# A second form of the first expert product for superblocks of at most 128 rows

## The chip, the cores and the metric

The kernel runs on one core of one Trainium2 chip. The metric is the device time of one execution in microseconds, lower is better. It is written in Tile, which places all semaphores; the order of the instructions of the part that matters here is the order of the source (manual_schedule).

## The reference

Pooled attention makes x (4608 rows of 512), a dense layer with softplus follows, and then a mixture of eight experts, which is the part of the change:

```python
do_compute = x @ w_skip > 0
e_idx = argmax(x[do_compute] @ w_gate, axis=1)
for e in range(8):
    h = maximum(xc[mask] @ w1[e], 0.0)
    y[mask] = gate_w[mask, None] * (h @ w2[e])
out[do_compute] = xc + y
```

Here w1[e] is 512 x 1024 and w2[e] 1024 x 512. Rows that are not computed are copied.

## The kernel before, in words

The first stage (attention and the dense layer, lines 93 to 734) ends where the experts' first matmul starts, 976.4 us into the span. The rows of each expert are cut into superblocks of at most 256 rows (SB), and a list of superblocks is made on the device. The first ten (list 1, NS1) are full ones that can start early; list 2 holds the rest, unrolled for up to 17 and left when a count n2 is reached (L836). The same word n2 has a bit for each superblock of list 2 that says whether it has more than 128 rows (L321 to L329). Superblocks are numbered through from 0, so list 2 begins with number 10.

A product of two float32 matrices is made of three matmuls: each operand is split into a part rounded to float32r and the rest (h and l), and hh, hl and lh are added in PSUM.

One superblock i (L748 to L807) does in this order:

- POOL issues the indirect DMAs that prepare what follows: w1 of superblock i+1 into raw1 (L759), the rows of i+2 into xg (L763), row numbers of i+3 (L765), and behind split2 w2 of i+1 into raw2 (L770). Where the expert doesn't change, the weights' indices lie out of bounds and nothing is moved.
- If superblock i has another expert than the one before, split2 (L388 to L394) makes w2h (ACT) and w2l (DVE) from raw2 in four pieces, inside a conditional (L767).
- The hidden product: 4 pairs of 128 features, each with 2 x 12 matmuls of 128x128 weights (w1h or w1l stationary) against 256 columns of x (L780). A pair ends in one PSUM tile h of the pool ps_f, which has four buffers; ACT makes hh with Relu (L784) and DVE hl (L785).
- turn(i+1) (L360 to L371): eight transposes of the next superblock's rows on PE, two copies to xth on ACT (L369), two subtractions to xtl on DVE (L370).
- If superblock i+1 has another expert, split1 (L380 to L386) makes w1h and w1l in four pieces, inside a conditional (L790).
- For each half j of 128 rows, the second product: 24 matmuls with 128 columns of hh or hl stationary and 512 columns of w2h or w2l moving (L799 to L801), a last sum on DVE (L803), and the indirect DMA of 128 rows to out on POOL (L805). In list 2 the second half stands inside a conditional on the bit (L795).

The program stands once for every superblock. Every engine with work in a conditional tests it itself; the page and the views put such instructions at lines like L767, L790, L793, L795 and L836, as COMPARE_BRANCH, ALU_OP and EVENT_SEMAPHORE on an engine's queue (PEldq, ACTq, DVEq, POOLq).

Of the kernel before, what the change touches and what calls it, by code (L numbers as in the profile page):

```python
# [9 lines left out]
F32 = mybir.dt.float32  # L10
# [4 lines left out]
AF = mybir.ActivationFunctionType  # L15
ALU = mybir.AluOpType
# [4 lines left out]
P = 128  # L21
# [7 lines left out]
SB = 256  # L29
# [5 lines left out]
def tile_kernel(ctx, tc, qT, kT, vT, wbits, w9, w1, w2, out):  # L35
    nc = tc.nc
# [23 lines left out]
    ident = const.tile([P, P], F32, name="ident")  # L60
# [37 lines left out]
    ws = {}  # L98
# [106 lines left out]
    misc = [None, 0]  # L205
# [134 lines left out]
    xg, xth, xtl = [None] * 3, [None] * 2, [None] * 2  # L340

    def at(i):
        return (lists[1], i) if i < NS1 else (lists[2], i - NS1)
# [8 lines left out]
    def gather(i):  # L352
        rows = NTOK - G if i < NS1 else NTOK
        for j in range(2):
            nc.gpsimd.indirect_dma_start(  # L355
                out=xg[i % 3][j], out_offset=None, in_=x2d[:rows, :],
                in_offset=bass.IndirectOffsetOnAxis(ap=ids[i % 4][:, j:j + 1], axis=0),
                bounds_check=rows - 1, oob_is_err=False)

    def turn(i, ps, tag):  # L360
        for half in range(2):
            tr = ps.tile([P, 512], F32, tag=tag, name="tr").rearrange("p (a b) -> p a b", a=2)
            for k2 in range(2):
                kk = half * 2 + k2
                for j in range(2):
                    nc.tensor.transpose(tr[:, k2, j * P:(j + 1) * P],  # L366
                                        xg[i % 3][j][:, kk * P:(kk + 1) * P], ident)
            h = xth[i % 2][:, half * 2:half * 2 + 2, :]
            nc.scalar.activation(out=h, in_=tr, func=AF.Copy)  # L369
            nc.vector.tensor_tensor(out=xtl[i % 2][:, half * 2:half * 2 + 2, :], in0=tr,  # L370
                                    in1=h.bitcast(F32), op=ALU.subtract)  # L371

    def fetch(name, src, i):
        li, s = at(i)
        nc.gpsimd.indirect_dma_start(  # L375
            out=ws[name], out_offset=None, in_=src,
            in_offset=bass.IndirectOffsetOnAxis(ap=li["widx"][:, s:s + 1], axis=0),
            bounds_check=NE * P - 1, oob_is_err=False)
# [18 lines left out]
    def wtile(name, *shape, dtype=F32):  # L397
        return wpool.tile([P, *shape], dtype, tag="w", name=name)

    with ExitStack() as ph:  # L400
# [10 lines left out]
        for i in range(2):  # L411
            t = ep.tile([P, 2 * SP], F32, name=f"kbd{i}")
# [229 lines left out]
        wl = load_weights()  # L642
# [72 lines left out]
        for i in range(2):  # L715
            t = xp.tile([P, 4 * G], F32R, tag="xl" if i == 0 else "xh", name=f"xt{i}")
            t = t[:, :4 * SB].rearrange("p (a b) -> p a b", a=4)
# [4 lines left out]
        hs = wtile("hs", 2, 8, SB, dtype=F32R)  # L722
        hh, hl = hs[:, 0], hs[:, 1]
# [3 lines left out]
        t = xp.tile([P, 4 * G], F32, tag="xl", name="xg1")  # L727
# [9 lines left out]
    ps_t = ctx.enter_context(tc.tile_pool(name="ps_t", bufs=2, space=PSUM))  # L737
    ps_f = ctx.enter_context(tc.tile_pool(name="ps_f", bufs=4, space=PSUM))
# [4 lines left out]
    t = ex.tile([P, 2 * XW], F32, name="xg2")  # L743
    xg[2] = [t[:, j * XW:(j + 1) * XW] for j in range(2)]
    nc.gpsimd.memset(t, 0.0)
    ys = [ex.tile([P, D], F32, name=f"ys{j}") for j in range(2)]

    def superblock(i, cond, mask, more, big=None):  # L748

        _, s = at(i)  # L750

        def changes(s_):
            return (mask & (1 << s_)) > 0

        with ExitStack() as st:
            if cond is not None:
                st.enter_context(tc.If(cond))
            if more > 0:
                fetch("raw1", w1, i + 1)  # L759
            if i == 0 and more > 0:  # L760
                gather(1)
            if more > 1:
                gather(i + 2)  # L763
            if more > 2:
                load_ids(i + 3)  # L765
            if i > 0 and i != NS1 - 1:
                with tc.If(changes(s)):  # L767
                    split2()
            if more > 0:
                fetch("raw2", w2, i + 1)  # L770
            xh, xl = xth[i % 2], xtl[i % 2]
            for fp in range(4):
                h = ps_f.tile([P, 2, SB], F32, tag="h", name="h")
                for f2 in range(2):
                    f0 = (fp * 2 + f2) * P
                    n = 0
                    for kk in range(4):
                        wh, wl = ws["w1h"][:, kk, f0:f0 + P], ws["w1l"][:, kk, f0:f0 + P]
                        for l, r in ((wh, xh), (wh, xl), (wl, xh)):
                            nc.tensor.matmul(h[:, f2, :], lhsT=l, rhs=r[:, kk, :],  # L780
                                             start=n == 0, stop=n == 11)
                            n += 1
                fs = slice(fp * 2, fp * 2 + 2)
                nc.scalar.activation(out=hh[:, fs, :], in_=h, func=AF.Relu)  # L784
                nc.vector.scalar_tensor_tensor(out=hl[:, fs, :], in0=h, scalar=0.0,  # L785
                                               in1=hh[:, fs, :].bitcast(F32),
                                               op0=ALU.max, op1=ALU.subtract)
            if more > 0:
                turn(i + 1, ps_t, "t")
                with tc.If(changes(s + 1)):  # L790
                    split1()
            for j in range(2):
                with ExitStack() as half:  # L793
                    if j and big is not None:
                        half.enter_context(tc.If((big & (32 << s)) > 0))  # L795
                    y = ps_o.tile([P, D], F32, tag=f"y{j}", name=f"y{j}")
                    js = slice(j * P, (j + 1) * P)
                    for f in range(8):
                        nc.tensor.matmul(y, lhsT=hh[:, f, js], rhs=ws["w2h"][:, f, :], start=f == 0, stop=False)  # L799
                        nc.tensor.matmul(y, lhsT=hh[:, f, js], rhs=ws["w2l"][:, f, :], start=False, stop=False)  # L800
                        nc.tensor.matmul(y, lhsT=hl[:, f, js], rhs=ws["w2h"][:, f, :], start=False, stop=f == 7)  # L801
                    r = xg[i % 3][j]
                    nc.vector.scalar_tensor_tensor(out=ys[j], in0=y, scalar=r[:, D:D + 1],  # L803
                                                   in1=r[:, :D], op0=ALU.mult, op1=ALU.add)
                nc.gpsimd.indirect_dma_start(  # L805
                    out=out, out_offset=bass.IndirectOffsetOnAxis(ap=ids[i % 4][:, j:j + 1], axis=0),
                    in_=ys[j], in_offset=None, bounds_check=NTOK - 1, oob_is_err=False)  # L807
# [77 lines left out]
```

## Time and profile before

| | us |
|---|---|
| median of 3 runs | 1439.58 |
| lowest and highest | 1439.39 to 1444.45 |
| profiled execution | 1446.33 |
| its span | 1444.6 |

The profile is of one execution. Start times count from the start of its span; 1.7 us of the profiled execution lie around the span. A matmul's duration is its latency: back-to-back matmuls overlap, so their cost is read from start to start. The granted clock of TensorE over the span is 0.998 of the full one.

### The profile page before, as it was taken

Reading aid. Unit: us, or ns where it says so; the run is one execution under the profiler, and the core shown is the slowest. Engines: PE = TensorE matmul, PEld = TensorE weight load, DVE = VectorE, ACT = ScalarE, POOL = GpSimd, SP = SyncE. Lnnn points to the kernel's source line nnn. Section 1 sums busy time; section 2 is a strip of 40 time slices with the busy share of each in tenths; the row PEclk is TensorE's granted clock in tenths of the full one; section 3 lists DMA queues with packets and bytes.
Section 4 is the critical chain, followed back from the end, with each engine's and each line's share of the span. In section 5 each row is a group of like instructions: output and inputs, shape, how many; then the busy total and the mean of one; then the engine's idle time right before and its main releaser. Section 6 shows DMA issues by size and latency. Waiting matters only on the chain. (4 is left out here: it accounts for less than half of the span.)

```text
span 1444.6 us, 21443 instructions
## 1 busy us (share of the span) xinstructions
PE 1402.9 (97%) x7434; PEld 1156.7 (80%) x7434; DVE 843.1 (58%) x2053; ACT 647.8 (45%) x1204; POOL 309.0 (21%) x365
## 2 busy tenths in 40 slices
PE   5999999999999999999999999999999999999996
PEld 3666877777877777777777777889898989999896
DVE  7898784784783883963963945753453422224254
ACT  5888654555554554555555444551111111113142
POOL 2010021021011121121120020134242433323232
PEclk9999999999999999999999999999999999999999
DMA  5445231231140130230310200502122111114051
GB/s 204 155 153 175 87 106 48 54 105 34 46 122 24 60 108 25 71 96 25 90 61 8 81 31 18 186 25 75 52 60 74 46 46 45 52 36 163 25 225 67
DMA packets 57691, 114.19 MB, mean 79 GB/s; under 512 B 17205, under 2 KB 23477, under 8 KB 56544
## 3 DMA queue, kind: packets, MB, share of 16 engines
q1 hardware_dynamic: 40032, 76.07, 17.0%
q0 software_dynamic: 17536, 36.60, 7.6%
q8 instruction: 62, 1.02, 0.3%
q14 instruction: 61, 0.50, 0.1%
HBM read 166.14 MB, written 29.67 MB: 136 GB/s over the span
## 5 line engine op out<-in xcount | busy, mean ns | idle before, releaser
L617 PE MATMUL h<-xh,wt 128*128 128x512 f32 x1152 | 390.4, 399 | 1.5 <-ACT wt L462 0.6
L617 PEld LDWEIGHTS h<-xh,wt 128*128 128x128 f32 x1152 | 216.6, 189 | 61.1 <-issue 11.5
L118 DVE CUSTOM_DVE_ANT_0 junk<-rows,w9b 128x512 bf16<-128x512 f32 x324 | 230.8, 712 | 10.2 <-ACT rows L112 3.8
L638 PE MATMUL y<-wt,gh 128*128 128x512 f32 x576 | 231.4, 402 | 2.4 <-ACT gh L625 2.2
L780 PE MATMUL h<-xt,w1h 128*128 128x256 f32 x1280 | 229.1, 281 | 2.7 <-PEq L793 1.0
L617 PE MATMUL h<-xl,wt 128*128 128x512 f32 x576 | 228.1, 396 | 0.0
L640 PE MATMUL y<-wt,gl 128*128 128x512 f32 x576 | 227.9, 396 | 0.0
L639 PE MATMUL y<-wt,gh 128*128 128x512 f32 x576 | 227.8, 396 | 0.0
L780 PEld LDWEIGHTS h<-xt,w1h 128*128 128x128 f32 x1280 | 198.3, 190 | 5.1 <-issue 1.4
L623 DVE SCALAR_TENSOR_TENSOR a<-h,a 128x512 f32<-128x512 f32 x144 | 99.0, 688 | 175.3 <-ACT a L622 169.5
L784 ACT ACTIVATE hs<-h 128x512 fp32r<-128x512 f32 x80 | 47.8, 598 | 330.8 <-PE h L780 268.8
L620 ACT ACTIVATE a<-h 128x512 f32<-128x512 f32 x144 | 86.2, 599 | 236.0 <-PE h L617 219.7
L780 PE MATMUL h<-xt,w1l 128*128 128x256 f32 x640 | 179.9, 281 | 0.7 <-DVEq L830 0.7
L531 POOL TENSOR_TENSOR q<-q,st 64x144 f32<-64x144 f32 (+7 forms) x60 | 60.7, 1019 | 533.4 <-DVE st L530 172.0
L625 ACT ACTIVATE gh<-a 128x512 fp32r<-128x512 f32 x144 | 90.8, 630 | 105.7 <-DVE a L623 103.9
L785 DVE SCALAR_TENSOR_TENSOR hs<-h,hs 128x512 fp32r<-128x512 f32 x80 | 54.6, 691 | 141.6 <-ACT hs L784 129.5
L638 PEld LDWEIGHTS y<-wt,gh 128*128 128x128 f32 x576 | 108.3, 188 | 29.0 <-ACT gh L625 3.3
L640 PEld LDWEIGHTS y<-wt,gl 128*128 128x128 f32 x576 | 108.3, 188 | 26.6 <-DVE gl L627 0.6
L617 PEld LDWEIGHTS h<-xl,wt 128*128 128x128 f32 x576 | 108.6, 189 | 23.5 <-issue 1.9
L639 PEld LDWEIGHTS y<-wt,gh 128*128 128x128 f32 x576 | 108.4, 188 | 23.6
L780 PEld LDWEIGHTS h<-xt,w1l 128*128 128x128 f32 x640 | 121.5, 190 | 0.9 <-DVEq L830 0.9
L799 PE MATMUL y<-w2h,hs 128*128 128x512 f32 x304 | 120.3, 396 | 0.4 <-ACT hs L784 0.4
(181 smaller groups left out, 1973.8 us busy)
## 6 DMA issues: line engine op xcount, KB each, us to landing
w9b<-w SPq DMA_DIRECT2D x81, 256.0 KB
raw<-wbits SPq DMA_DIRECT2D x32, 512.0 KB
x2d<-rows SPq DMA_DIRECT2D x36, 260.0 KB
kv<-kT SPq DMA_DIRECT2D x28, 288.0 KB
kv<-vT SPq DMA_DIRECT2D x28, 288.0 KB
q<-qT SPq DMA_DIRECT2D x8, 224.0 KB
q<-qT SPq DMA_DIRECT2D x8, 192.0 KB
q<-qT SPq DMA_DIRECT2D x8, 160.0 KB
```

Source lines behind the costliest of these rows:

```text
L118: nc.vector.tensor_tensor_reduce(out=ws["junk"], in0=rows[t][:, :D], in1=w9b[e], scale=1.0, scalar=0.0, op0=ALU.mult, op1=ALU.add, accum_o ...
L531: nc.gpsimd.tensor_tensor(out=ep_, in0=ep_, op=ALU.mult, in1=rc[:tp, h].unsqueeze(2).to_broadcast([tp, 2 * nt, SP]))
L617: nc.tensor.matmul(h, lhsT=l, rhs=r[:, kk, :], start=n == 0, stop=n == 11)
L620: nc.scalar.activation(out=a, in_=h, func=AF.Abs)
L623: nc.vector.scalar_tensor_tensor(out=a, in0=h, scalar=0.0, in1=a, op0=ALU.max, op1=ALU.add)
L625: nc.scalar.activation(out=gh, in_=a, func=AF.Copy)
L638: nc.tensor.matmul(y, lhsT=th, rhs=wh, start=c == 0, stop=False)
L639: nc.tensor.matmul(y, lhsT=th, rhs=wl, start=False, stop=False)
L640: nc.tensor.matmul(y, lhsT=tl, rhs=wh, start=False, stop=c == 15)
L780: nc.tensor.matmul(h[:, f2, :], lhsT=l, rhs=r[:, kk, :], start=n == 0, stop=n == 11)
L785: nc.vector.scalar_tensor_tensor(out=hl[:, fs, :], in0=h, scalar=0.0, in1=hh[:, fs, :].bitcast(F32), op0=ALU.max, op1=ALU.subtract)
L799: nc.tensor.matmul(y, lhsT=hh[:, f, js], rhs=ws["w2h"][:, f, :], start=f == 0, stop=False)
```

## The change

The hidden product moves into a function hidden, as it was. A second function, hidden_small, takes the 128 rows of x as the stationary operand and 512 features of w1 as the moving one, 24 matmuls in all, and leaves the Relu of the result, rows on partitions, in hr, a free part of the tile misc. hidden_turn then transposes hr in eight pieces of 128x128 and makes hh and hl from the PSUM tiles. List 1 calls hidden, as before. In list 2 each superblock has two conditionals on the bit: one with hidden and turn, one with hidden_small, turn and hidden_turn.

```diff
--- before.py
+++ after.py
@@ -745,6 +745,53 @@
     nc.gpsimd.memset(t, 0.0)
     ys = [ex.tile([P, D], F32, name=f"ys{j}") for j in range(2)]
 
+    hr = misc[0][:, 3072:4096].rearrange("p (a b) -> p a b", b=P)
+    assert misc[1] <= 1024
+
+    def hidden(i):
...
+    def hidden_small(i):
+
+        xh, xl = xth[i % 2], xtl[i % 2]
+        for half in range(2):
+            h = ps_f.tile([P, 4, P], F32, tag="h", name="hs")
+            fs = slice(half * 512, half * 512 + 512)
+            n = 0
+            for kk in range(4):
+                wh, wl = ws["w1h"][:, kk, fs], ws["w1l"][:, kk, fs]
+                for l, r in ((xh, wh), (xl, wh), (xh, wl)):
+                    nc.tensor.matmul(h.rearrange("p a b -> p (a b)"), lhsT=l[:, kk, :P], rhs=r,
+                                     start=n == 0, stop=n == 11)
+                    n += 1
+            nc.scalar.activation(out=hr[:, half * 4:half * 4 + 4, :], in_=h, func=AF.Relu)
+
+    def hidden_turn():
+        for half in range(2):
+            fs = slice(half * 4, half * 4 + 4)
+            tr = ps_f.tile([P, 4, P], F32, tag="h", name="ht")
+            for f in range(4):
+                nc.tensor.transpose(tr[:, f, :], hr[:, half * 4 + f, :], ident)
+            nc.scalar.activation(out=hh[:, fs, :P], in_=tr, func=AF.Copy)
+            nc.vector.tensor_tensor(out=hl[:, fs, :P], in0=tr, in1=hh[:, fs, :P].bitcast(F32),
+                                    op=ALU.subtract)
+
     def superblock(i, cond, mask, more, big=None):
 
         _, s = at(i)
@@ -768,25 +815,22 @@
                     split2()
             if more > 0:
                 fetch("raw2", w2, i + 1)
...
+            if big is None:
+                hidden(i)
+                if more > 0:
+                    turn(i + 1, ps_t, "t")
+            else:
+
+                with tc.If((big & (32 << s)) > 0):
+                    hidden(i)
+                    if more > 0:
+                        turn(i + 1, ps_t, "t")
+                with tc.If((big & (32 << s)) < 1):
+                    hidden_small(i)
+                    if more > 0:
+                        turn(i + 1, ps_t, "t")
+                    hidden_turn()
             if more > 0:
-                turn(i + 1, ps_t, "t")
                 with tc.If(changes(s + 1)):
                     split1()
             for j in range(2):
```

## Rows read from the trace of the kernel before

**Rows 1.** The page, busy time, share of the span and instructions.

```profile
PE 1402.9 (97%) x7434; PEld 1156.7 (80%) x7434; DVE 843.1 (58%) x2053; ACT 647.8 (45%) x1204; POOL 309.0 (21%) x365
```

**Rows 2.** The page, costliest groups: line, operation, shapes, count | busy us, mean ns | idle before.

```profile
L780 PE MATMUL h<-xt,w1h 128*128 128x256 f32 x1280 | 229.1, 281 | 2.7 <-PEq L793 1.0
...
L784 ACT ACTIVATE hs<-h 128x512 fp32r<-128x512 f32 x80 | 47.8, 598 | 330.8 <-PE h L780 268.8
...
L799 PE MATMUL y<-w2h,hs 128*128 128x512 f32 x304 | 120.3, 396 | 0.4 <-ACT hs L784 0.4
```

**Rows 3.** Timeline of PE, superblocks 17, 18, start of 19: start us, us, instruction [idle, releaser].

```profile
1373.12 0.40 PE L780 MATMUL h<-xt,w1h 128*128 128x256 f32 x2
...
1384.44 1.03 PE L366 MATMUL tr<-ident,xg 128*128 128x128 f32 x8
...
1385.23 0.48 PE L799 MATMUL y<-w2h,hs 128*128 128x512 f32 x1
...
1390.57 0.39 PE L801 MATMUL y<-w2h,hs 128*128 128x512 f32 x1
...
1391.98 0.48 PE L780 MATMUL h<-xt,w1h 128*128 128x256 f32 x2 [1.02 <-PEq L793]
...
1409.69 0.39 PE L801 MATMUL y<-w2h,hs 128*128 128x512 f32 x1
...
1411.06 0.47 PE L780 MATMUL h<-xt,w1h 128*128 128x256 f32 x2 [0.98 <-ACT w1h L384]
```

**Rows 4.** Timeline, PE and DVE, superblock 19.

```profile
1423.36 0.40 PE L801 MATMUL y<-w2h,hs 128*128 128x512 f32 x1
...
1423.51 1.28 DVE L370 TENSOR_TENSOR xt<-tr,xt 128x512 fp32r<-128x512 f32 x2
```

**Rows 5.** Line 790 in superblock 19: duration ns min/median/max, first and last start.

```profile
L790 DVEq EVENT_SEMAPHORE  x1: 21/21/21, 1424.8 to 1424.8; - x1
```

**Rows 6.** Line 793 at the end of superblock 17, PE's queue.

```profile
L793 PEldq COMPARE_BRANCH  x1: 210/210/210, 1386.8 to 1386.8; - x1
...
L793 PEldq EVENT_SEMAPHORE  x1: 51/51/51, 1391.0 to 1391.0; - x1
```

**Rows 7.** Timeline, waits released by another engine's conditional, superblocks 10 and 18.

```profile
1210.78 0.39 PE L780 MATMUL h<-xt,w1l 128*128 128x256 f32 x1 [0.67 <-DVEq L830]
...
1391.14 3.90 ACT L392 ACTIVATE w2h<-raw 128x1024 fp32r<-128x1024 f32 x4 [1.09 <-PEq L793]
```

**Rows 8.** Line 767 at the head of superblock 17, DVE's queue.

```profile
L767 DVEq EVENT_SEMAPHORE  x1: 21/21/21, 1374.1 to 1374.1; - x1
```

**Rows 9.** Timeline, ACT, DVE and POOL, superblocks 17 to 19.

```profile
1385.18 1.08 ACT L369 ACTIVATE xt<-tr 128x512 fp32r<-128x512 f32 x2
...
1393.07 4.63 DVE L393 TENSOR_TENSOR w2l<-raw,w2h 128x1024 fp32r<-128x1024 f32 x4 [0.53 <-DVEq L793]
...
1398.89 1.05 POOL L375 DMA_INDIRECT raw<-w,misc  x1 [0.30 <-ACT hs L784]
...
1407.57 3.91 ACT L384 ACTIVATE w1h<-raw 128x1024 fp32r<-128x1024 f32 x4
...
1414.58 2.01 ACT L392 ACTIVATE w2h<-raw 128x1024 fp32r<-128x1024 f32 x2 [3.10 <-DMA raw<-w,misc]
```

**Rows 10.** Stretches: length, busy us (count) by engine, granted clock, DMA share, GB/s.

```profile
1388.00:1390.00 2.00, 2.00 (x11) 1.65 (x10) 2.00 (x3) 2.00 (x3) 0.00 (x0) 1.00 0.52 221
...
1412.00:1414.00 2.00, 2.00 (x20) 2.00 (x20) 1.97 (x3) 0.00 (x0) 0.00 (x0) 1.00 0.23 90
...
1438.00:1440.00 2.00, 0.00 (x0) 0.00 (x0) 0.00 (x0) 0.00 (x0) 0.00 (x0) 0.53 0.02 4
```

**Rows 11.** Groups by shape, line 507 (scores; boot is the start of the kernel).

```profile
L507 PE MATMUL s<-kbd,q 128*128 128x144 f32 x128 | 18.4, 286 | 0.0
...
L507 PE MATMUL s<-kbd,boot 128*128 128x144 f32 x32 | 9.1, 466 | 14.0 <-ACT raw L456 6.9 <-ACT kbd L504 5.1 <-DVE boot L520 2.0
```

**Rows 12.** Chain of waits, list 2: an output of 128 rows.

```profile
1414.25 2.34 DMA out<-ys,ids
```

More of the change, by code (lines that the diff above doesn't have):

```diff
@@ L746, in tile_kernel @@
     ys = [ex.tile([P, D], F32, name=f"ys{j}") for j in range(2)]
+    hr = misc[0][:, 3072:4096].rearrange("p (a b) -> p a b", b=P)
+    assert misc[1] <= 1024
+    def hidden(i):
+        xh, xl = xth[i % 2], xtl[i % 2]
+        for fp in range(4):
+            h = ps_f.tile([P, 2, SB], F32, tag="h", name="h")
+            for f2 in range(2):
+                f0 = (fp * 2 + f2) * P
+                n = 0
+                for kk in range(4):
+                    wh, wl = ws["w1h"][:, kk, f0:f0 + P], ws["w1l"][:, kk, f0:f0 + P]
+                    for l, r in ((wh, xh), (wh, xl), (wl, xh)):
+                        nc.tensor.matmul(h[:, f2, :], lhsT=l, rhs=r[:, kk, :],
+                                         start=n == 0, stop=n == 11)
+                        n += 1
+            fs = slice(fp * 2, fp * 2 + 2)
+            nc.scalar.activation(out=hh[:, fs, :], in_=h, func=AF.Relu)
+            nc.vector.scalar_tensor_tensor(out=hl[:, fs, :], in0=h, scalar=0.0,
+                                           in1=hh[:, fs, :].bitcast(F32),
+                                           op0=ALU.max, op1=ALU.subtract)
+    def hidden_small(i):
+        xh, xl = xth[i % 2], xtl[i % 2]
+        for half in range(2):
+            h = ps_f.tile([P, 4, P], F32, tag="h", name="hs")
+            fs = slice(half * 512, half * 512 + 512)
+            n = 0
+            for kk in range(4):
+                wh, wl = ws["w1h"][:, kk, fs], ws["w1l"][:, kk, fs]
+                for l, r in ((xh, wh), (xl, wh), (xh, wl)):
+                    nc.tensor.matmul(h.rearrange("p a b -> p (a b)"), lhsT=l[:, kk, :P], rhs=r,
+                                     start=n == 0, stop=n == 11)
+                    n += 1
+            nc.scalar.activation(out=hr[:, half * 4:half * 4 + 4, :], in_=h, func=AF.Relu)
[8 more added lines that the diff above has]
+                                    op=ALU.subtract)
     def superblock(i, cond, mask, more, big=None):
@@ L770, in superblock @@
                 fetch("raw2", w2, i + 1)
[L771 to L787, printed above, removed]
+            if big is None:
[12 more added lines that the diff above has]
+                    hidden_turn()
             if more > 0:
-                turn(i + 1, ps_t, "t")
                 with tc.If(changes(s + 1)):
```

## The prediction

> **What bounds the kernel now.** I read the page's busy table first: PE is busy 97% of the span [rows 1], so a gain must shorten PE's own row of work, and a loss comes from anything that opens a gap in it. The table of costliest groups then counts what the changed part runs: 1280 first-product matmuls are 64 to a superblock (w1h against two halves of x), so 20 superblocks, and 304 matmuls at L799 are 8 to a half, so 38 halves: two superblocks run one half [rows 2]. The timeline shows which: 17 and 18 have one y half between their hidden products [rows 3]. Only they can take the new short form. Superblocks 10 to 16 and 19, eight of them, are in the second list too: they get both new tests and keep the old work. Superblocks 0 to 9 are untouched.
>
> **The short form, PE alone.** Superblock 17's hidden product takes 1373.12 to 1384.44, 11.3 us, the eight transposes of turn 0.79, the 24 y matmuls of 512 columns 5.34 from first to last start, 0.23 each [rows 3]. The new product is 24 matmuls of that width, 24 x 0.23 = 5.5, and eight more 128x128 transposes, 0.8. Saved on PE alone: 11.3 - 6.3 = 5.0 a superblock, 10 us in all. That is the ceiling.
>
> **The eight big superblocks.** This is where I think the change loses. A conditional body that is skipped still has to raise the semaphores that its work would have raised. The trace shows it as an EVENT_SEMAPHORE on each engine that has work in the body, and it fires in order, when that engine has finished what came before. At the end of superblock 17 PE tested L795's condition at 1386.8, four microseconds early, but its event waited until 1391.0, when the last y matmul was through [rows 6], and the next matmul began 1.02 us after the drain [rows 3]. Others wait for such events: split2's first copy on ACT was released by PE's event of L793, and PE at superblock 10 by DVE's event of L830 [rows 7]. After the change hh and hl are written last, in program order, by hidden_turn inside the second conditional. In a big superblock that body is skipped, so y's first matmuls must wait for ACT's and DVE's events there, and those come only when ACT and DVE are through with everything in the first body, turn's copies included. Today's L790 events are the same point: in superblock 19 DVE's is at 1424.8 [rows 5], right behind the turn subtraction that ends at 1424.79 [rows 4]. The first y matmul that reads hl started at 1423.36 [rows 4]; it would start just after 1424.8, 1.45 us later, plus 0.1 to 0.2 for the weight load that can no longer be pulled ahead (at L830 PE started 0.06 us after the event). I take 1.6. The bounds are 0.8 (PE's own drain alone: the 1.02 seen, less the further tests that follow it there) and 1.75. Nothing hides it, since PE has no other gap in these superblocks for it to replace. 8 x 1.6 = 12.8 us. Behind the waiting weight load queue the rest of y and the next product on PE, and behind them DVE's last sum, the output's DMA and the next fetches on POOL: all of it moves later together. In a big superblock the first body ends in a jump, as L793's body does wherever it is taken, and that shows no gap; it costs nothing while PE's sequencer runs ahead.
>
> **Superblock 17.** The first body is skipped. The PSUM tiles of the short form take the places of the skipped h tiles, so PE waits for ACT's and DVE's events. DVE has just finished y's last sum of superblock 16; its event at L767 is at 1374.1 [rows 8], the new one some 0.3 later: PE starts at 1374.5 instead of 1373.12. Product to 1380.0, turn to 1380.8, new transposes to 1381.6. ACT does the second Relu (0.6 [rows 2]), two turn copies, then the first new copy (0.54 each, half of the 1.08 for two [rows 9]), until 1382.4; DVE the two turn subtractions (1.28 for two [rows 4]) and the first new one, until 1383.5. y's third matmul starts at 1383.6, the last 21 x 0.23 later at 1388.4, against 1390.57 [rows 3]. Gain 2.2, of 5.0.
>
> **Superblock 18.** It changes expert, so ACT and DVE do split2 at its head, ahead of the new test in their program. PE waits for their events behind that. raw2's traffic stops at 1389.0 (52% of the stretch from 1388 [rows 10]); for superblock 19 ACT, which waited for the data, started 2.1 us after the traffic ended (1414.58 against 23% of the stretch from 1412 [rows 9, 10]), so I take 1391.1 as the landing, just where ACT starts today [rows 7]. The shorter 17 does not bring it forward, since its fetch was issued at 17's head. DVE follows the first copy by some 1.1 and needs 4.63 for its four pieces [rows 9]: done at 1396.9. PE then starts at 1397.1 instead of 1391.98. By 17's pattern (13.9 us from first to last matmul) the last y matmul starts at 1411.0, against 1409.69 [rows 3]: 1.3 later, all that 17 won and more. Superblock 19 starts that much later; its weights come earlier than now, as POOL's queue follows 17's output.
>
> PE would stand idle for 8 us in front of superblock 18. The granted clock shows the price: when PE has no work left the clock is 0.53 from 1438 on, down at the lower of its levels (1.2 against 2.4 GHz) [rows 10]. At the start of the kernel the score matmuls after such pauses take 466 ns, the same form later 286 [rows 11], though the clock column has 1.00 there. Bounds: nothing, or all 24 matmuls at half speed, 5.5; I take 2.0, a little over a third of them. By the clock column at the start nothing would be lost, and the sum below would be 14.1. The Trainium skill ("TensorE: Matmul & The Clock Gate", Part 1) says that the throttled state is the default and that activity releases it; by that rule the matmuls at the start, and the first ones behind this wait, run slow whatever the column says. The 466 against 286 ns agree with the rule, the column does not.
>
> **Sum.** 12.8 - 2.2 + 3.5 + 2.0 = 16.1 us later. The profiled execution took 1446.33 (span 1444.6), the median of the runs is 1439.58, so the profiled one is 6.7 above; I put the difference on the median: 1455.6. About 0.5% (7.2 us) is what a measurement of this kernel can tell from no change.
>
> **Rivals.**
> *The skipped bodies cost only their tests (chance 0.10).* No event is waited for, by PE or from it. Then 17 and 18 win 5.0 each, less 1.5 each because y waits for the last copies, and 19 waits for its weights: their fetch, behind 17's output on POOL, is issued at 1398.89 today [rows 9], 3.5 earlier then; it lands within 8.7 (split1 begins at 1407.57 [rows 9]), and 2.3 for the first piece on ACT and DVE make 1406.4, where PE would be ready at 1411.06 - 7.0 = 1404.1. Net -7.0 + 2.3 = -4.7: 1434.9, not slower; at best, with the weights in time and the copies hidden, -10, and half of this chance I put beyond the bound of 0.5%. The tests are free while PE's sequencer is ahead (4 us at L793). Against: rows 6 and 7. It decides if y's first matmul in a big superblock follows turn's transposes without a gap. The Trainium skill ("Advanced Engine Details and Errata", Control Flow Timing) gives about 108 ns for a compare-and-branch; by it alone 20 tests would be an estimated 2.2 us, and the change would come out 2.5 us ahead. The rows say otherwise, as the gap is made by the event and not by the test.
>
> *PE drains, but nobody else is waited for (0.13).* 8 x 0.8 = 6.4, less the 4.7: +1.7, 1441.3. For it: the 1.0 gap of PE behind L793 is sure [rows 3, 6]. Against: PE's wait for DVE at L830 [rows 7].
>
> *Each skip leaves the fetched code (0.11).* The skipped bodies are 80 and 208 PE instructions long; L793's is 48 and shows no more than the drain. If PE must fetch code after each skip, at the 2.3 us of a small transfer in the chain [rows 12], some 1.5 us of it beyond the wait eight times and 2.3 twice, this adds 16.6: 1472.
>
> *The change does not do what it says:* excluded, since the two one-half superblocks are there, and the bit that skips their second half is the one the new tests read.
>
> **Numbers.** The forecast has 0.66 and its own range is 1451 (1.45 a superblock, no clock loss, raw2 1.6 earlier: 11.6 - 2.2 + 1.9) to 1460 (1.75, and the clock for all 24: 14.0 - 2.2 + 9.0). The range 1441 to 1470 also takes in the drain case and the lower part of the fetch case. Slower by over 0.5%: 0.65 of the forecast and 0.11, 0.76. Within: 0.13, half of the first rival and the forecast's edge, 0.19. Faster: 0.05.
>
> **What would show it.** In the timeline of superblocks 10 to 16, a gap of some 1.6 us on PE between turn's transposes and y's third matmul, released by DVE's event of the second new test; in 17 a late start of 1.4 and last y start near 1388 plus the 11.2 of the seven before; in 18 a PE gap of about 8 us that ends with split2's last subtraction, with a granted clock below 1.00. The prediction is wrong if the big superblocks keep their length, or if 18's product starts before split2 is over. If the gaps are longer than 3 us and no engine's event ends them, it is the fetch.

## The result, and the profile after

The kernel after takes 1461.53 us (median of 4 runs, 1460.85 to 1462.35) against 1441.75 before (4 runs, 1439.39 to 1444.45): a ratio of 1.014, with the interval from 1.012 to 1.016, so slower by 17 to 23 us. The profiled execution took 1460.85, its span is 1458.9.

The place is the second list. I measure it from the last y start of superblock 9 to that of superblock 19, in the timeline of PE: 241.5 us against 224.1, 17.4 more. The rest of the two spans differs by 3 us the other way, in work that the change doesn't touch. The table gives the lengths of the list and of four superblocks for every kernel of this study, in its profiled execution, each from one last y start to the next; the ratio is that to the kernel before on the same chip.

| kernel | 11 (big) | 17 (short) | 18 (short) | 19 (big) | list 2 | ratio, 95% interval |
|---|---|---|---|---|---|---|
| before | 23.12 | 17.68 | 19.12 | 23.90 | 224.1 | |
| after | 24.72 | 15.65 | 25.01 | 26.14 | 241.5 | 1.014 (1.012 to 1.016) |
| first_only | 23.12 | 17.68 | 19.23 | 24.44 | 224.9 | 0.999 (0.998 to 1.001) |
| second_full | 24.70 | 19.27 | 21.37 | 28.27 | 243.7 | 1.012 (1.008 to 1.016) |
| second_short | 24.70 | 19.26 | 21.36 | 29.86 | 245.3 | 1.012 (1.009 to 1.015) |
| second_no_hh | 24.21 | 18.68 | 20.34 | 26.84 | 236.0 | 1.009 (1.006 to 1.012) |
| turn_behind | 23.58 | 14.98 | 24.86 | 24.62 | 231.6 | 1.005 (1.003 to 1.007) |
| split2_inside | 24.93 | 16.16 | 22.16 | 28.93 | 243.6 | 1.014 (1.011 to 1.017) |
| both | 23.72 | 15.26 | 20.35 | 26.67 | 230.1 | 1.005 (1.003 to 1.007) |
| else_form | 24.05 | 14.12 | 17.02 | 29.92 | 231.2 | 1.005 (1.003 to 1.006) |
| else_turn | 23.14 | 13.36 | 16.66 | 29.83 | 223.5 | 0.9995 (0.998 to 1.001) |
| else_turn_out | 23.12 | 13.36 | 18.18 | 24.64 | 219.7 | 0.995 (0.994 to 0.997) |
| warm | 24.84 | 16.39 | 22.92 | 28.33 | 242.7 | one run |
| before_out | 23.12 | 17.68 | 19.06 | 24.30 | 224.5 | 1.000 (0.999 to 1.001) |

The page of the kernel after, busy times:

```profile
PE 1399.9 (96%) x7306; PEld 1146.2 (79%) x7306; DVE 840.7 (58%) x2049; ACT 647.5 (44%) x1204; POOL 309.5 (21%) x365
```

Against [rows 1] PE has 128 matmuls fewer, two times 96 - 24 - 8, and 3 us less to do, and the span is 14.3 longer. The time lies in gaps. The waits of PE in the second list name them (total us, times, longest):

```profile
PE hs L780 <- DVEq L824: 9.9, 2, 8.5
PE y L843 <- ACTq L828: 6.8, 8, 0.9
PE y L845 <- DVEq L828: 1.8, 8, 0.2
```

Lines 824 and 828 are the two new conditionals. Eight times, once in each big superblock, y's first and third matmul wait for events of the second one; twice the short product waits for an event of the first one. Superblock 12 in the timeline of PE and DVE, and the rows of line 828 there (duration in ns, first and last start):

```profile
1268.85 1.03 PE L366 MATMUL tr<-ident,xg 128*128 128x128 f32 x8
1270.28 1.28 DVE L370 TENSOR_TENSOR xt<-tr,xt 128x512 fp32r<-128x512 f32 x2
1270.72 0.50 PE L843 MATMUL y<-w2h,hs 128*128 128x512 f32 x1 [0.84 <-ACTq L828]
...
1271.67 0.50 PE L845 MATMUL y<-w2h,hs 128*128 128x512 f32 x1 [0.23 <-DVEq L828]
```

```profile
L828 ACTq EVENT_SEMAPHORE  x1: 17/17/17, 1270.7 to 1270.7; - x1
...
L828 DVEq EVENT_SEMAPHORE  x1: 21/21/21, 1271.6 to 1271.6; - x1
```

In [rows 3] y starts 0.79 behind the transposes; here it is 1.87, when ACT's event has come, and the third matmul starts at 1271.67, when DVE's has. DVE's event stands right behind the turn subtraction, which ends at 1271.56. The body of line 828 is skipped here. Nobody works in it, and still everyone who reads hh or hl waits until ACT and DVE have finished what is in front of it.

The timeline of PE, superblocks 17, 18 and the start of 19:

```profile
1381.25 0.39 PE L845 MATMUL y<-w2h,hs 128*128 128x512 f32 x1
1383.02 0.71 PE L780 MATMUL hs<-w1h,xt 128*128 128x512 f32 x2 [1.39 <-DVEq L824]
...
1388.70 1.03 PE L366 MATMUL tr<-ident,xg 128*128 128x128 f32 x8
...
1396.90 0.39 PE L845 MATMUL y<-w2h,hs 128*128 128x512 f32 x1
1405.77 1.19 PE L780 MATMUL hs<-w1h,xt 128*128 128x512 f32 x2 [8.48 <-DVEq L824]
...
1421.91 0.39 PE L845 MATMUL y<-w2h,hs 128*128 128x512 f32 x1
1423.51 0.47 PE L761 MATMUL h<-xt,w1h 128*128 128x256 f32 x2 [1.20 <-issue]
```

The gap of 8.48 us in front of 18 is the largest of the kernel's second list. DVE's row for split2, and the events of the first conditional's line, say what ends it:

```profile
1400.94 4.63 DVE L393 TENSOR_TENSOR w2l<-raw,w2h 128x1024 fp32r<-128x1024 f32 x4 [0.93 <-ACT w2h L392]
```

```profile
L824 DVEq EVENT_SEMAPHORE  x2: 21/21/21, 1382.9 to 1405.6; - x2
```

split2's last subtraction ends at 1405.57, the event comes at 1405.6, PE starts at 1405.77. And stretches there, with the granted clock as the third number from the end:

```profile
1400.00:1402.00 2.00, 0.00 (x0) 0.00 (x0) 1.07 (x2) 2.00 (x3) 1.04 (x1) 0.65 0.07 25
1402.00:1404.00 2.00, 0.00 (x0) 0.00 (x0) 2.00 (x3) 1.75 (x2) 0.21 (x1) 0.50 0.16 60
1408.00:1410.00 2.00, 2.00 (x6) 1.57 (x5) 0.00 (x0) 0.00 (x0) 1.41 (x2) 0.50 0.88 336
1412.00:1414.00 2.00, 2.00 (x12) 1.64 (x11) 0.00 (x0) 0.05 (x1) 0.00 (x0) 1.00 0.92 384
```

The clock falls to the lower level (1.2 against 2.4 GHz) while PE stands, and is still there from 1408 to 1410: there the matmuls follow each other at 0.43 us, and from 1411 on at 0.23. (The twelve of the last row include the first short transposes.)

### The profile page after: what moved, and what is told of

It reads as the page before. It is cut to its first block, busy times and chain, and to the rows that moved or that the text cites. A ratio compares the mean times of both kernels' runs of the same rounds, so it can differ in the third digit from the quotient of the medians.

```text
span 1458.9 us, 21336 instructions
## 1 busy us (share of the span) xinstructions
PE 1399.9 (96%) x7306; PEld 1146.2 (79%) x7306; DVE 840.7 (58%) x2049; ACT 647.5 (44%) x1204; POOL 309.5 (21%) x365
## 5 line engine op out<-in xcount | busy, mean ns | idle before, releaser
L617 PEld LDWEIGHTS h<-xh,wt 128*128 128x128 f32 x1152 | 216.6, 189 | 60.9 <-issue 11.3
L761 PE MATMUL h<-xt,w1h 128*128 128x256 f32 x1152 | 206.5, 281 | 1.9 <-issue 1.2
L620 ACT ACTIVATE a<-h 128x512 f32<-128x512 f32 x144 | 86.2, 599 | 235.9 <-PE h L617 219.7
L761 PEld LDWEIGHTS h<-xt,w1h 128*128 128x128 f32 x1152 | 178.7, 190 | 3.9 <-issue 1.6
L765 ACT ACTIVATE hs<-h 128x512 fp32r<-128x512 f32 x72 | 43.1, 599 | 309.8 <-PE h L761 269.6
L761 PE MATMUL h<-xt,w1l 128*128 128x256 f32 x576 | 162.0, 281 | 0.7 <-DVEq L874 0.7
L843 PE MATMUL y<-w2h,hs 128*128 128x512 f32 x304 | 120.3, 396 | 7.7 <-ACTq L828 6.8
L845 PE MATMUL y<-w2h,hs 128*128 128x512 f32 x304 | 119.6, 393 | 2.2 <-DVEq L828 1.8
L847 DVE SCALAR_TENSOR_TENSOR ys<-y,xg 128x512 f32<-128x512 f32 x38 | 28.5, 751 | 161.1 <-PE y L845 161.1
```

Source lines behind the costliest of these rows:

```text
L617: nc.tensor.matmul(h, lhsT=l, rhs=r[:, kk, :], start=n == 0, stop=n == 11)
L620: nc.scalar.activation(out=a, in_=h, func=AF.Abs)
L761: nc.tensor.matmul(h[:, f2, :], lhsT=l, rhs=r[:, kk, :], start=n == 0, stop=n == 11)
```

## The experiments

The theory: a conditional body that is skipped costs its in-order events, 1.6 us in each big superblock through the second new conditional, and the wait for split2 in 18 through the first. The rivals: each engine pays for fetching code behind a skip, by the length of the body; only PE's drain costs; the tests cost; or the short form itself is slow. The edits below are against the kernel after, unless another is named.

**first_only: one conditional, always entered.** The second one and its body are left out, so the short superblocks do the long form's work.

```diff
-                with tc.If((big & (32 << s)) > 0):
+                with tc.If((big & 31) > 0):
                     hidden(i)
...
-                with tc.If((big & (32 << s)) < 1):
-                    hidden_small(i)
...
-                    hidden_turn()
```

> In list 2 one conditional that is always entered stands around the hidden product and turn, and there is no second one; every superblock takes the old 256-column form. Theory (only a skipped body costs, because its events come late): the ten entered conditionals cost nothing, and the time is that of the kernel before within 2 us, near 1442, with no gap between turn's transposes and y. Rival (the tests and the jump out of a body cost, or the loss of the finer waits at the end of any conditional): 0.8 to 1.6 us a superblock on ten superblocks, 8 to 16 us more, 1450 to 1458.

Superblock 11 takes 23.12 us, to the hundredth that of before, and the ratio is 0.999. The timeline of PE there:

```profile
1245.25 1.04 PE L366 MATMUL tr<-ident,xg 128*128 128x128 f32 x8
1246.04 0.48 PE L838 MATMUL y<-w2h,hs 128*128 128x512 f32 x1
```

0.79 between the two, as in [rows 3]. Here a test and a body that is entered cost nothing that can be measured.

**second_full, second_short, second_no_hh: a second conditional that is never entered.** In all three hidden and turn run unconditionally in every superblock; the skipped body is the whole short form, or hidden_turn alone, or hidden_small alone, which writes neither hh nor hl.

```diff
-                with tc.If((big & (32 << s)) > 0):
-                    hidden(i)
...
+                hidden(i)
+                if more > 0:
+                    turn(i + 1, ps_t, "t")
-                with tc.If((big & (32 << s)) < 1):
+                with tc.If((big & 31) > 30):
                     hidden_small(i)
                     if more > 0:
                         turn(i + 1, ps_t, "t")
                     hidden_turn()
```

> In list 2 the old hidden product and turn stand unconditionally; behind them stands one conditional that is never entered, with the whole new body (short product, turn, transposes and copies to hh and hl). No superblock uses the short form. Theory: y's first matmuls wait in all ten superblocks for ACT's and DVE's events of the skipped body, 1.6 us each, 16 us more than before: about 1458. Rival drain (only PE's own event): 0.8 each, 1450. Rival fetch (code behind a long skip): 16 us too, but then the next kernel, with a short body, falls to 1450.

> As the kernel with the never entered second conditional, but its body is only the eight new transposes with their copies to hh and hl, 16 PE instructions instead of some 80. No superblock uses the short form. Theory (events of ACT and DVE, which come when turn's copies are through, however long the body): unchanged, 1.6 us in each of ten superblocks, about 1458, the gap before y's third matmul released by DVE's event. Rival fetch: the skip is short, so the gap falls to PE's drain, 0.8 each, about 1450.

> As the kernel with the never entered second conditional, but its body is only the short product with its Relu into hr: nothing in it writes hh or hl, which y reads. 48 PE instructions are skipped. No superblock uses the short form. Theory: y no longer waits for ACT's or DVE's events, only PE's own event is left, which comes when turn's last transpose is through: some 0.8 us in each of ten superblocks, 8 us more than before, about 1450. Rival (the waits of y are not what costs, any skip costs the same): 16 us, 1458. Rival (PE's event costs nothing): 1442.

The full body and the short one both give 24.70 in superblock 11. So the length of the skipped body doesn't matter there, and code fetching is out. Their timelines of PE there show the two waits of the kernel after; second_short first, then second_full:

```profile
1246.24 0.50 PE L839 MATMUL y<-w2h,hs 128*128 128x512 f32 x1 [0.84 <-ACTq L827]
...
1247.19 0.50 PE L841 MATMUL y<-w2h,hs 128*128 128x512 f32 x1 [0.22 <-DVEq L827]
```

```profile
1247.81 0.50 PE L842 MATMUL y<-w2h,hs 128*128 128x512 f32 x1 [0.84 <-ACTq L827]
...
1248.77 0.50 PE L844 MATMUL y<-w2h,hs 128*128 128x512 f32 x1 [0.22 <-DVEq L827]
```

Without a write of hh and hl in the body 24.21 are left: the wait for ACT and DVE is gone, and PE's own drain remains. It is 1.09 us, not 0.8, and the list is 11.9 longer than before where I expected 8. The timeline of PE, and PE's rows of line 827 (the skipped conditional) and line 830 (split1's, which comes next):

```profile
1247.98 1.03 PE L366 MATMUL tr<-ident,xg 128*128 128x128 f32 x8
1249.68 0.47 PE L839 MATMUL y<-w2h,hs 128*128 128x512 f32 x1 [0.67 <-DVE hs L766]
```

```profile
L827 PEldq EVENT_SEMAPHORE  x1: 51/51/51, 1249.1 to 1249.1; - x1
```

```profile
L830 PEldq COMPARE_BRANCH  x1: 215/215/215, 1249.3 to 1249.3; - x1
```

The releaser that the timeline names is not the one: that subtraction ended at 1249.55 and writes hl, which y's first matmul doesn't read, and in superblocks 11 to 18 y starts 0.17 us behind the end of line 830's test, however far from the subtraction. PE tested line 827 at 1246.9, ahead of its work, but its event came when the transposes were through, 1249.1, and only then could it test line 830, 1249.3, with 0.2 us for the test. So a test is free as long as PE's sequencer is ahead, and not free behind an event.

Superblock 19 stands apart in all three: 28.27, 29.86 and 26.84 against 23.90. ACT's last Relu comes late there, and with it y. In second_short it starts 3.1 us behind the first transpose (0.3 in the kernel before), and y waits longest:

```profile
1439.38 0.50 PE L839 MATMUL y<-w2h,hs 128*128 128x512 f32 x1 [3.71 <-ACTq L827]
```

In second_full and second_short the clock also falls behind this wait (0.50 from 1442 to 1444 in second_full). Why the Relu is late is not shown, and for 19 no rival is excluded.

**turn_behind: the turn behind both conditionals.**

```diff
                     hidden(i)
-                    if more > 0:
-                        turn(i + 1, ps_t, "t")
                 with tc.If((big & (32 << s)) < 1):
                     hidden_small(i)
-                    if more > 0:
-                        turn(i + 1, ps_t, "t")
                     hidden_turn()
+                if more > 0:
+                    turn(i + 1, ps_t, "t")
```

> The changed kernel with turn(i+1) taken out of both conditionals of list 2 and put behind them. In a big superblock the events of ACT and DVE in the skipped second body then come when the last Relu and its remainder are through, some 1.7 us after the last product matmul, while PE drains and does turn's transposes (0.8). Theory: y no longer waits for them, PE's own drain of 1.1 us (the body that writes no hh: 24.20 against 23.12 us a superblock) is what stays, so eight big superblocks lose 1.1 instead of 1.6, 4 us less than the changed kernel, and the two short ones gain some 0.8 each, since ACT makes hh before turn's copies: near 5 to 6 us less than the changed kernel, 1.0% above the kernel before instead of 1.4%. Rival (the waits do not hang on turn's copies): the same as the changed kernel.

Superblock 11 takes 23.58, the whole ratio is 1.005: half of what I expected to be left. The timeline of PE in superblock 12:

```profile
1268.45 1.06 PE L366 MATMUL tr<-ident,xg 128*128 128x128 f32 x8 [0.30 <-PEq L826]
1269.27 0.48 PE L841 MATMUL y<-w2h,hs 128*128 128x512 f32 x1
```

ACT's and DVE's events now come before the turn copies and are covered by the eight transposes, as no wait for them is left in front of y. PE's drain is still there, but costs 0.46 and not 1.1, since the transposes stand directly behind the event with no test between, and the next test runs under them. Superblock 18 keeps its gap (8.94 us, by DVE's event of line 824).

**split2_inside: split2 in the first body, and behind the short form in the second.** raw2's fetch, which may overwrite what split2 reads, goes behind both.

```diff
-            if i > 0 and i != NS1 - 1:
-                with tc.If(changes(s)):
-                    split2()
-            if more > 0:
-                fetch("raw2", w2, i + 1)
...
                 with tc.If((big & (32 << s)) > 0):
+                    with tc.If(changes(s)):
+                        split2()
                     hidden(i)
...
                     hidden_turn()
+                    with tc.If(changes(s)):
+                        split2()
+                if more > 0:
+                    fetch("raw2", w2, i + 1)
```

> The changed kernel with split2 of list 2 moved into the two bodies: ahead of the old product in the first, behind hidden_turn in the second, and the fetch of raw2 behind both. Theory: in superblock 18 DVE's event of the skipped first body no longer stands behind split2, so PE's gap there falls from 8.5 to some 1.4 us, as in superblock 17, the clock is not lost (24 matmuls in 5.7 instead of 7.9 us), and y of 18 is paced by split2 instead; 18 gets 6 to 8 us shorter, the big superblocks keep their 1.6. The fetch for superblock 19 is issued later, which may give back 1 to 3. Sum: 4 to 8 us less than the changed kernel, 0.9 to 1.1% above the kernel before. Rival (the gap in 18 is the wait for the weights themselves, wherever the split stands): PE idle moves in front of y and the time stays within 2 us of the changed kernel.

I expected 4 to 8 us less than the kernel after, and there are none: 1.014 again. PE in front of 18, then at 18's y, then POOL's fetch of raw2 for 19:

```profile
1404.20 0.70 PE L780 MATMUL hs<-w1h,xt 128*128 128x512 f32 x2 [3.07 <-DVEq L824]
```

```profile
1415.17 0.50 PE L849 MATMUL y<-w2h,hs 128*128 128x512 f32 x1 [1.89 <-ACT w2h L392]
```

```profile
1420.56 1.23 POOL L375 DMA_INDIRECT raw<-w,misc  x1 [7.05 <-ACT w1h L384]
```

The gap of 8.48 is 3.07 (DVE's event now stands behind split1's last piece and 17's last sum), and the clock fell all the same: 0.50 from 1406 to 1408, and the 24 matmuls took 7.17 us. split2 then stands in front of y instead, which waits 1.89 for it. 18 wins 2.85. But 17 loses 0.5 and each big superblock 0.2, because w2l has a conditional writer behind the second test too, and 19 loses 2.8, because raw2's fetch for it goes out only at 1420.56, 2.4 us ahead of 18's last y start (11.0 ahead in the kernel after, at 1410.89): y's second matmul waits 1.30 for DVE's event behind that late split2, and the clock is 0.50 once more from 1440 to 1442. The work was moved from one wait into four others. The rival had this time, within 2 us of the kernel after, and PE's idle in front of y; but the gap in front of 18 did shrink.

**both: the two edits together.**

> The two moves together: split2 inside the bodies, turn and the fetch of raw2 behind both conditionals. Theory: the two gains add, 10 to 13 us less than the changed kernel, 0.3 to 0.6% above the kernel before; the eight drains of PE (1.1 each, 9 us) are left and are more than the two short superblocks win. Rival (drains are free once nothing else waits): below the kernel before by up to 5 us.

1.005, as turn_behind alone. Of the 4.5 us that 18 wins over turn_behind, 2.05 are lost in 19, 0.3 in 17 and 0.1 in each of the seven big ones ahead of it; the list is 1.5 shorter, which the ratio can't show. With two plain conditionals the change stays slower than before.

**else_form: the second conditional as the first one's Else.**

```diff
-                with tc.If((big & (32 << s)) > 0):
+                with tc.If((big & (32 << s)) > 0) as cmp:
...
-                with tc.If((big & (32 << s)) < 1):
+                with cmp.Else():
```

> The changed kernel with the second conditional written as the Else of the first, nothing else. One engine then runs either body and is brought to a common count at the end. Theory: events are still needed where the bodies differ in their counts, PE at least has to make up the difference, and y has to wait for a count that holds for both bodies; between the kernel before plus 9 us (drain alone) and the changed kernel. If the events come only on the path with the smaller count (the short one), the big superblocks lose nothing and the time is at or below the kernel before. The timeline of superblocks 10 to 16 decides: 24.7, 24.2 or 23.1 us each.

This separates the events from the rest. The trace has no EVENT_SEMAPHORE on either line, and the short product of 17 starts with no gap. The timeline of PE in 11, and at the head of 17, 18 and 19:

```profile
1240.94 0.50 PE L843 MATMUL y<-w2h,hs 128*128 128x512 f32 x1 [0.30 <-ACT xt L369]
```

```profile
1373.23 0.63 PE L780 MATMUL hs<-w1h,xt 128*128 128x512 f32 x2
...
1389.10 0.70 PE L780 MATMUL hs<-w1h,xt 128*128 128x512 f32 x2 [1.59 <-ACT w1h L384]
...
1407.58 0.51 PE L761 MATMUL h<-xt,w1h 128*128 128x256 f32 x2 [3.05 <-ACT w1h L384]
```

17 and 18 are now 3.6 and 2.1 below before. But big superblocks keep 0.9, since y's first matmul waits for turn's first copy on ACT (0.30 of idle) and its third, 0.84 behind it, for turn's first subtraction on DVE. And 19 loses 6: its weights aren't there when the shorter 18 ends, and then the clock falls:

```profile
1410.00:1412.00 2.00, 2.00 (x11) 2.00 (x11) 2.00 (x2) 0.37 (x1) 0.00 (x0) 0.50 0.56 229
```

**else_turn: the Else form, and the turn behind both bodies.** This is else_form with the diff of turn_behind.

> The Else form with turn(i+1) behind it. In the Else form a big superblock took 24.05 us (23.13 before) and y waited for turn's copies on ACT, with no event and no drain of PE; the short superblocks started without waiting for events, and 18 kept its clock (24 matmuls in 5.6 us). Theory: with turn behind, y and turn wait for the last Relu and its remainder at most, which come while turn's transposes run: 0 to 0.5 us a big superblock instead of 0.9, so 0 to 4 us, against 3 to 5 us won by the two short ones: between 0.3% below and 0.1% above the kernel before. Rival (a wait at the end of the Else costs PE a drain wherever it stands): 0.5 and more a superblock, 0.2 to 0.4% above the kernel before, as with two conditionals and turn behind.

Now a big superblock takes 23.14 and costs nothing, 17 wins 4.3 and 18 wins 2.5. The ratio is still 0.9995: 19 takes 29.83, 5.9 more than before. Its wait in the timeline of PE, the stretch behind it, and POOL's issues of 17's second output and of the fetch for 19's first weights:

```profile
1401.49 0.51 PE L761 MATMUL h<-xt,w1h 128*128 128x256 f32 x2 [4.01 <-ACT w1h L384]
```

```profile
1403.00:1405.00 2.00, 2.00 (x10) 2.00 (x11) 2.00 (x3) 1.28 (x2) 0.00 (x0) 0.50 0.95 401
```

```profile
1389.22 1.82 POOL L847 DMA_INDIRECT out<-ys,ids  x1 [2.54 <-DVE w2l L393]
1391.34 1.04 POOL L375 DMA_INDIRECT raw<-w,misc  x1 [0.30 <-ACT hs L791]
```

The fetch stands on POOL behind the output of 17's empty second half, and that issue waited 2.54 us. (The row names split2 on DVE; in second_full and split2_inside the same issue waits 2.46, and the row names the landing of the first output.)

**else_turn_out: the output's DMA inside the half's own conditional.** The empty half then issues none.

```diff
-                nc.gpsimd.indirect_dma_start(
-                    out=out, out_offset=bass.IndirectOffsetOnAxis(ap=ids[i % 4][:, j:j + 1], axis=0),
-                    in_=ys[j], in_offset=None, bounds_check=NTOK - 1, oob_is_err=False)
+                    nc.gpsimd.indirect_dma_start(
+                        out=out, out_offset=bass.IndirectOffsetOnAxis(ap=ids[i % 4][:, j:j + 1], axis=0),
+                        in_=ys[j], in_offset=None, bounds_check=NTOK - 1, oob_is_err=False)
```

> As the one with the Else form and turn behind it, and the output DMA of the second half is issued inside that half's conditional, so that the short superblocks don't issue it and POOL doesn't wait there for the first half's output to land. Theory: in the Else form superblock 19 waited 3.05 + 0.76 us for its first weights, whose fetch stands on POOL behind that wait (3.6 us in superblock 17 of the kernel before); it goes, and 19 starts 3 to 4 us earlier: 0.2 to 0.5% below the kernel before. Rival (POOL's own events of the skipped conditional, or traffic, hold the fetch up as long): no gain over the kernel it is made from.

POOL's fetch, and the head of 19 on PE:

```profile
1387.59 1.43 POOL L375 DMA_INDIRECT raw<-w,misc  x1 [0.69 <-ACT w2h L392]
```

```profile
1400.65 0.47 PE L761 MATMUL h<-xt,w1h 128*128 128x256 f32 x2 [1.30 <-ACT w1h L384]
```

The fetch leaves 4.1 us earlier, counted from 17's last y start. 19 waits 1.30 instead of 4.01, its second wait is gone, the clock stays at the upper level, and it takes 24.64. But 18 takes 1.5 more. In both kernels ACT does split2 ahead of the product's Relu, and PE's transposes of the result wait for that. PE in 18 and a stretch behind the wait, in else_turn:

```profile
1390.00 1.15 PE L790 MATMUL ht<-ident,misc 128*128 128x128 f32 x8 [1.99 <-ACT misc L783]
```

```profile
1391.00:1393.00 2.00, 2.00 (x15) 1.75 (x14) 1.85 (x4) 1.81 (x4) 1.39 (x3) 1.00 0.06 13
```

The same in else_turn_out:

```profile
1390.24 1.15 PE L790 MATMUL ht<-ident,misc 128*128 128x128 f32 x8 [1.90 <-ACT misc L783]
```

```profile
1391.00:1393.00 2.00, 2.00 (x13) 2.00 (x12) 1.85 (x4) 1.67 (x3) 1.39 (x3) 0.59 0.98 410
```

The waits are alike; the clock falls behind the second and not behind the first. So the loss at the lower clock has moved from 19 into 18, and what the edit wins is 19's waits. The list takes 219.7, 4.4 less than before, and the ratio is 0.995 (0.994 to 0.997): 1438.5 against 1445.8 (medians of 12 and 23 runs). The other 2.9 us between these medians lie outside the list, and no run here places them. This version beats both kernels, the one before by half a per cent.

**before_out: the kernel before with that last edit alone.**

> The kernel before with one edit: the output DMA of the second half stands inside that half's conditional. It is the control for the fastest kernel so far (Else form, turn behind, output inside; ratio 0.9953). Theory: in the kernel before, superblock 19 does not wait for its weights but for PE's own event (0.98 us), so an earlier fetch wins nothing: 0 to 1 us, ratio 0.999 to 1.001, and the gain of that kernel is the short form's, which only the earlier fetch lets come through. Rival (the output's place alone makes the gain, as POOL is freed everywhere): 4 to 7 us less, ratio 0.995 to 0.997.

1.000 (0.999 to 1.001). The place of the output gains nothing by itself; the gain of else_turn_out in the list is the short form's, and the edit keeps 19 from giving it back.

**warm: PE kept busy in front of 18.** 28 matmuls of 512 columns, whose results are unused, in front of 18's short product. PE waits 2.35 us ahead of the first of them, and then they run until the product starts, 9.24 us behind 17's last y start (8.87 in the kernel after).

```diff
         xh, xl = xth[i % 2], xtl[i % 2]
+        if i == NS1 + 8:
+            y1 = ps_o.tile([P, D], F32, tag="y1", name="warm")
+            for n in range(28):
+                nc.tensor.matmul(y1, lhsT=xh[:, n % 4, :P],
+                                 rhs=xh[:, 0:2, :].rearrange("p a b -> p (a b)"), start=True, stop=True)
```

> The changed kernel, with 28 matmuls of 512 columns into an unused PSUM tile ahead of the short product of superblock 18 alone; their results are not used. They fill PE's 8.5 us of waiting for split2's event. Theory: the wait ends at the same time, but the 24 matmuls of the short product then take 5.6 us, as in superblock 17, instead of 7.9, with a granted clock of 1.00: superblock 18 is 2.2 us shorter. Rival (the 7.9 us are waits for weights and not the clock): they still take 7.9.

The timeline of PE, the first of the added matmuls, the product's first row and the row behind its last:

```profile
1402.65 6.66 PE L776 MATMUL warm<-xt 128*128 128x512 f32 x28 [2.35 <-DVEq L842]
...
1409.15 0.62 PE L785 MATMUL hs<-w1h,xt 128*128 128x512 f32 x2
...
1414.60 1.04 PE L366 MATMUL tr<-ident,xg 128*128 128x128 f32 x8
```

The 24 matmuls take 5.45 us, against 7.92 in the kernel after (1405.77 to 1413.69) and 5.68 in 17. So 2.2 to 2.5 us of 18 are the clock's, and 18 as a whole is 2.1 shorter. It is no gain for the kernel: 17 and 19 are 0.7 and 2.2 longer in this one run. The trace shows where: y's first matmul waits 1.39 us for ACT in 17, where it was 0.47, and 2.14 in 19, where it was 0.84:

```profile
1438.56 0.53 PE L848 MATMUL y<-w2h,hs 128*128 128x512 f32 x1 [2.14 <-ACTq L833]
```

Behind that the clock is 0.50 from 1440 to 1442. Why ACT is late there is not shown.

## Why the prediction was right

The direction and the places were right, and the time lies in the range of 1441 to 1470. It is not as near as the steps: 1461.53 is 5.9 above the 1455.6 and outside the 1451 to 1460 that the forecast gave itself. Of the 5.9, 2.2 are the base (1439.58 was the median of three runs before, 1441.75 is that of four), 1.3 the list and 2.4 neither. Step by step:

- **Eight big superblocks, 12.8 forecast.** Right. 10 to 16 are 11.3 longer together, 1.6 each. The waits are those of the forecast: ACT's and DVE's events of the second conditional, DVE's right behind the turn subtraction. first_only takes the second conditional away and the cost is gone; second_short puts it back alone and the cost is there.
- **Superblock 17, -2.2.** Right: 15.65 against 17.68, -2.03. From the start of the product to y's third matmul 9.0 us were measured, 9.1 forecast.
- **Superblock 18, +3.5 and +2.0 for the clock.** Right: +5.9. The start lies 8.87 us behind 17's last y start (8.7 forecast), and the end of split2's last subtraction releases it. The clock's part was the weakest term, taken between 0 and 5.5; it is 2.2 by 17's product and 2.5 by warm. That 2.0 came so near is luck, as no row told it from the two bounds. The Trainium skill ("TensorE: Matmul & The Clock Gate", Part 1) says that the clock is released by activity and throttled otherwise; the stretches here agree, and this time the clock column shows it, at 0.50. The 1.00 of that column at the start of the kernel, by which the sum would have been 14.1, was no good witness: from 36 to 38 us, with six matmuls in either trace, it has 1.00 in the kernel before and 0.50 in before_out.
- **Superblock 19.** +2.24, of which the forecast had 1.6. 0.2 more is its later start, and 0.4 a product of 11.4 instead of 11.0, which stays unexplained.
- **PE's drain alone, 0.8** (a bound, and the price in the second rival). Mis-sized: 1.09 where a test stands behind the event, 0.46 where it doesn't. In these two kernels it isn't one number: it goes with what follows the event.
- **The sum, 16.1.** The list shows 17.4, the medians 19.8 with the interval from 17 to 23. The 2.4 between list and medians lie outside the list or between runs, and I can't place them.

Of the rivals, code fetching is refuted in superblocks 10 to 18: a skipped body with 40 matmuls and transposes for PE (24 and 8 and 8), and one with 8, give the same 24.70 in 11 and agree to 0.1 in the others. "The skipped bodies cost only their tests" is what the Else form does: there 17 wins 4.3 and 18 wins 2.5, where the rival had 3.5 each, and 19 waits for its weights, 4.0 and 0.75 where it had 2.3; with the output out of the way the list wins 4.4, where it had 4.7, though of other parts: 17 wins 4.3 and 18 0.9, and 19 loses 0.7. For the plain second conditional it is false. The test's own price is visible only behind an event, 215 ns on PE in second_no_hh. The Trainium skill ("Advanced Engine Details and Errata", Control Flow Timing) has about 108 ns for a compare-and-branch, and the rows here don't bear out one figure: at line 827 there it is 217 ns on PE, 50 on ACT and 63 on DVE, and at line 824 of the kernel after PE's go from 68 to 338.

What stays open: why the Else form needs no events at its end, and why ACT is late in front of y in some superblocks from 17 on. The runs show that the Else form has no events, and that their cost goes; not by what means the order is kept there.

## What to carry to other kernels

In this kernel a conditional body that is skipped is paid for by every engine with work in it and by everyone who reads what it writes, because its events come in order. Write two alternatives as one If with an Else, and keep work that both share, like the turn here, behind them. When a stage gets shorter, look next at the transfers that its length had hidden, and at what stands in front of their issue on the queue; in else_turn that took 5.9 of the 6.8 us that the short form had won, until one needless output was out of the way. A wait of a few microseconds on TensorE can cost more than itself: behind the one of 8.48 the matmuls ran at the lower clock and lost another 2.2 to 2.5. So when a stage gets longer, read the clock column there before the edit is blamed, as in 18 of else_turn_out.

## What the runs showed of the hardware that was not expected

- Two conditionals with opposite tests, and one If with an Else, do the same work. In a big superblock they differ by 0.67 us with the turn inside (24.72 against 24.05) and by 0.44 with the turn behind (23.58 against 23.14), and the last of these is the time of before. The Else form shows no event on its lines.
- After 3.07 us without work the clock fell to 0.50 (split2_inside), and after 4.01 and 0.75 too (else_turn); behind the 1.39 in front of 17 the 24 matmuls took 5.68 us, close to the 5.45 of the busy PE in warm. I had taken a loss behind a gap of 8 us for likely, not behind one of 3. And the length of the pause alone doesn't tell: the clock fell behind 1.90 us in else_turn_out, and not behind 1.99 in else_turn or 2.35 in warm.
